# A fused attention and expert kernel: one exponential moved a pair sooner, the second pair's operands copied in three pieces, doubled filler products, and a new instruction order

## The chip, the cores and the metric

The kernel runs on one core of one Trainium2 chip. The metric is the time in microseconds (us) of one execution on the device, lower is better. The core's engines run side by side: TensorE (PE in the profile, with its weight loads as PEld), VectorE (DVE), ScalarE (ACT), GpSimd (POOL), and SyncE (SP), which issues DMAs. Results of products land in PSUM, in eight banks.

## The reference

Two steps, one behind the other. First soft-capped attention over 8 batches, 12 heads, 448 positions and 64 columns a head; then, on its output, four attention experts of 64 columns, of which each position uses two.

```python
def _attn_ref(q, k, v, cap):
    scores = np.matmul(q, k.transpose(0, 1, 3, 2)) / np.sqrt(64)
    scores = cap * np.tanh(scores / cap)              # cap = 30
    attn = softmax(scores)
    return np.matmul(attn, v)

def _moe_ref(x, w_gate, wq, wk, wv, wo):              # x: 8 x 448 x 768
    logits = x @ w_gate                               # 4 experts, the best 2 are used
    for e in range(4):
        a = softmax(causal(x @ wq[e] @ (x @ wk[e]).T / 8))
        ye = a @ (x @ wv[e]) @ wo[e]
        out += weight_of_e(logits) * ye
    return out
```

## The kernel before

**Attention** works on pairs of heads: 48 pairs (`NP`), six a batch (`HP`), and two more short ones (`NPV` is 50) for the last 128 positions of the last batch. For each pair the loop at the end of the kernel issues, in this order: loads (L486 keys, L495 queries, L490 tails), casts to 16 bits (`cast`, on POOL mostly), transposes on TensorE with one copy out of PSUM (`tr`, L711 and L701, copied at L752), score products (`fill`, L789 and L799), tanh on ACT (`tanh`, L842), one exp on ACT for all scores of a pair (`expo`, L854), products with the values (`pv`, L869 and L877), scaling on DVE, and a transpose into `xT`.

The scores of a pair come in three groups: X (three banks), Y1 and Y2 (the same two banks). A pair's tanh order is X, Y1, then the exp of the pair before, then Y2. Where a pair is not in `alone`, its Y2 products and the next pair's X products are one block in TensorE's order; a pair in `alone` gives them singly.

**The experts** of a batch are interleaved with the attention of the next batch: values, keys and queries (`b_v`, `b_qk`), the gate on POOL, two masks, and for each of the two chosen ranks a slot: score products and one exp of 1024 columns on ACT (`b_score`, L1158 and L1167), products with the values (`b_pv`, L1217, scaled on DVE at L1232), then sums on POOL (`b_ot`, L1242), transposes by DMA (L395) and output products (`b_wo`, L1279), stored at L1293. `exps` says which pair carries a slot: pairs 5 and 6 after a batch's first, and for batch 6 pairs 5 and 7, that is pairs 47 and 49. The last batch's experts (`last`, `last2`) follow at the end.

**The order** of each engine's instructions is worked out before anything is issued. Every operation is entered into a graph with an assumed duration and, in places, a due time counted from a tanh of ACT (`ref` and an offset). `solve` then simulates all engines and picks, on the engine that can start first, the operation with the lowest rank: its due time, changed by constants and by a jitter from `SEEDS` and `JIT`. Operations marked `first` (scores, transposes, operand copies) may pass ahead of the picked one when they are due soon. `LAND` is the time that the simulation assumes for a load to land. ACT's tanh and exp are chained in program order.

**Filler products** (L1589 at the start, L1644 behind each tanh of pairs 1 to 7) multiply zeros into a free bank.

Of the kernel before, what the change touches and what calls it, by code (L numbers as in the profile page):

```python
# [16 lines left out]
SWITCH = 0.1  # L17
WARM = 5.5
TAIL = 4
LAND = 2.942  # L20
LAND0 = 2.314
FLIGHT = 8
JIT = 0.377
SEEDS = (0, 0, 0, 641, 0, 564, 447, 0, 424, 0, 460, 0, 235, 957, 407, 782, 983, 0, 912, 404, 0, 970, 362, 0, 379, 864, 0, 72, 966, 0, 904, 104, 0, 980, 497, 974, 196, 827, 159, 0, 805, 165, 0, 235, 0, 755, 596, 262, 998, 26, 102, 0, 0, 552, 777, 594, 0, 873, 143, 97, 0, 0, 943, 0, 690, 925, 0, 147, 0, 0, 0, 830, 464, 0, 0, 0, 267, 0)
TWIRE = 0.1
BEGIN = {"POOL": 0.8, "DVE": 0.9, "SP": 0.8, "ACT": 0.8, "PE": 1.25}
NWARM = 6
KEEP = 8
KEEPN = 1
HEAD = 12.0  # L30
MD = 4
NAT = 36
# [21 lines left out]
class Graph:  # L54
# [79 lines left out]
    def solve(self, when, banks, lent):  # L134
# [44 lines left out]
        while len(order) < n:  # L179
            best = None  # L180
            for e, rs in ready.items():
                if not rs:
                    continue
                c = [(est(o, e), o) for o in rs if e == o.eng or not left]
                if not c:
                    continue
                t0 = min(x[0] for x in c)
                if t0 >= INF or (best is not None and t0 >= best[0]):
                    continue
                def rank(x):  # L190
                    u = x[1]
                    if u.name[:4] == "gexp":
                        return -INF, 0.0, 0
                    d = u.due + lag if u.first or left < TAIL else max(u.due + lag, t0 + 1.097)
                    d -= 0.796 * (u.grp is not None and not u.opens and left >= TAIL)
                    k = SEEDS[int(t0 / 4.0)] if t0 < 4.0 * len(SEEDS) else 0
                    if k:
                        d += ((u.idx * 40503 + k * 9973) % 1009 / 1009.0 - 0.5) * JIT
                    return d - 2.0 * (u.half == 1 and half == 1), u.due, u.idx

                near = t0 + (0.005 if left >= TAIL else SWITCH + 0.02)
                t, o = min((x for x in c if x[0] <= near), key=rank)
                early = e == "POOL" and t < HEAD
                if (e in ("PE", "DVE") or early) and not o.first:
                    for t2, u in c:
                        if u.first and u.due + lag < t + o.occ + 0.433 and t2 < t + (
                                o.occ if early else max(SWITCH + 0.01, min(o.occ, 0.25))):
                            t, o = t2, u
                            break
                if best is None or t < best[0]:  # L210
                    best = (t, e, o)
# [64 lines left out]
def kernel(  # L276
# [418 lines left out]
    def tr(p):  # L695
# [19 lines left out]
        if p == 0:  # L715
            gk, gq = Group(AUX), Group(AUX)
            pe(0, lambda: tk(gk, (1, 0, 2)), kr, [("tps", p, "k")], gk, occ=0.165, name=f"trk{p}")
            act(0.37, lambda: nc.scalar.copy(qk[t][:, S + 128 :], bank16(gk)[:, S + 128 : S + 512]),
                [("tps", p, "k")], [("qk", t, "k")], gk, fixed=True)
            pe(0, lambda: tq(gq, 0, 2), [("q16", i), "ident"], [("tps", p, "q")], gq, occ=0.1,  # L720
               name=f"trq{p}")
            pe(0, lambda: tq(gq, 2, 4), [("q16b",), "ident"], [("tps", p, "r")], gq, occ=0.1,
               name=f"trr{p}")
            dve(c_dve(S, True), lambda: nc.vector.tensor_copy(
                qk[t][:, 0:S], bank16(gq)[:, 0:S]), [("tps", p, "q"), ("tps", p, "r")], [("qk", t, "q")], gq,
                name="qk0")
            return
        g = Group(AUX)
        if p >= KD:
            pe(0, lambda: tq(g, 0, 2), [("q16", i), "ident"], [("tps", p, "q")], g, occ=0.1,  # L730
# [12 lines left out]
        pe(0, lambda: tk(g, (0, 1, 2)), kr + [("s", XB[0])] * (p == 1), [("tps", p, "k"), ("qkw", t)], g, occ=0.165, name=f"trk{p}")  # L743
        m, kx = (4, (-1,)) if p == 1 else (2, ())
        pe(0, lambda: (tq(g, 0, m), None if kx else tk(g, (-1,))),
           [("q16", i), "ident"] + (ktr if not kx else []),
           [("tps", p, "q")], g, occ=0.2 if kx else 0.15, name=f"trq{p}",
           due=5.0 if p == 1 else None)
        pe(0, lambda: tk(g, kx) if kx else tq(g, 2, 4), [("q16", i), "ident"] + (ktr if kx else []),
           [("tps", p, "r")], g, occ=0.06 if kx else 0.1, name=f"trr{p}" if p == 1 else "", due=5.0 if p == 1 else None)  # L750
        dve(c_dve(S + 512, True),
            lambda: nc.vector.tensor_copy(qk[t], bank16(g)[:, 0 : S + 512]),  # L752
            [("tps", p, x) for x in "kqr"], [("qk", t, "k"), ("qk", t, "q"), ("qk", t, "t")], g, name=f"qk{p}")
# [72 lines left out]
        return [o for o in G.ops if o.fixed][-1]  # L826

    XOFF = (5, 6)
    late = {6: (5, 7)}
    exps = {HP * (b + 1) + o: (b, s) for b in range(LB) for s, o in enumerate(late.get(b, XOFF))}  # L830
    alone = {0, *exps}
    ACTS = {}
    SL = {"X": (0, 3), "Y1": (3, 5), "Y2": (5, 7)}

# [148 lines left out]
    def b_v(b, ref):  # L983
        x = b % 2
        for n in range(4):
            g = Group(AUX + XB, 1.8)
            w = WIN[n]
            for j0 in (0, 2, 4):
                def mm(g=g, w=w, j0=j0):
                    for j in (j0, j0 + 1):  # L990
                        nc.tensor.matmul(  # L991
                            bank(g)[:, 0 : E * Dh + E], xT[x][:, j, w : w + 128], wvg[:, j, :],
                            start=(j == 0), stop=(j == NDC - 1),
                        )

                pe(0, mm, [("xT", x, j) for j in range(NDC)] + [("wvg", e) for e in range(E + 1)],
                   [("vps", b, n)], g, occ=0.22, name=f"v{b}_{n}",
                   due=(ref, 7.244 + 1.4 * n))
            lo = 64 if n == 3 else 0
            dve(0.08, lambda g=g, n=n: nc.vector.tensor_copy(  # L1000
                lg[x][:, (n + 1) % 4, :], bank(g)[:, E * Dh : E * Dh + E]),
# [6 lines left out]
    def b_qk(b, ref):  # L1008
        x = b % 2
        for r in range(2):  # L1010
            for which in "kq":
                g = Group(AUX + XB, 2.4)
                w2 = (wq2 if which == "q" else wk2)[r]
                for j in range(NDC):
                    def mm(g=g, w2=w2, j=j, which=which):
# [7 lines left out]
                    pe(S, mm, ([("mB", 0), ("mB", 1)] if which == "q" and b >= MD else []) + [("xT", x, i) for i in range(NDC)] + [  # L1023
                            (f"w{which}2", 2 * r), (f"w{which}2", 2 * r + 1)],
                        [(which, b, r)], g, name=f"{which}{b}_{r}",
                        due=(ref, 11.984 + 5.015 * r + 1.8 * (which == "q")))
                if which == "k":
                    dve(c_dve(S), lambda g=g, r=r: nc.vector.tensor_copy(
                        kB[x][r], bank(g)[:, 0:S]), [("k", b, r)], [("kB", x, r)], g, name=f"kB{b}")
# [334 lines left out]
    def last(ref):  # L1364
# [82 lines left out]
        for n in range(3):  # L1447
# [5 lines left out]
            def mm(g=g, n=n):  # L1453
                for e in range(E):
# [8 lines left out]
                ("vB", x, c) for c in range(n + 1)], [("pvL", n)], g, occ=0.12 * (n + 1),  # L1463
                name=f"pvL{n}")
            normed(n, g, view, ("pvL", n), (z[:, n].rearrange("p (e o) -> p e o", o=1),
                   [(b, 3, "z")]), None, WIN1[n], (ref, 9.616))
        last2(ref)

    def gate_tail(b, tag, g, ps, m, z, l, t, s_, key):
# [42 lines left out]
    def last2(ref):  # L1512
# [63 lines left out]
        for e in range(E):  # L1576
            pe(0, lambda e=e: pv_(e), [("p2", e), "vL"] + [("vB", x, c) for c in range(3)],
               [("pvL", 3)], g, occ=0.12, name="pvL3")
        normed(3, g, view, ("pvL", 3), (gt2[0].rearrange("p o e -> p e o"), [(b, 2, "z"), (b, 2, "s")]),
               gt2[3][:, 1, 0], W1, (ref, 9.108))  # L1580

# [14 lines left out]
    for p in range(NPV):  # L1596
# [13 lines left out]
        for what in order:  # L1610
            if what == "Y2" and p:
# [1 line left out]
                if p in exps:  # L1613
                    b_score(*exps[p])
                pv(p - 1)
                xt(p - 1, (ACTS["Y1", p], 3.335))
                if p % HP == 0 and p < NP:
                    bb = p // HP - 1
                    b_v(bb, ACTS["Y1", p])
# [88 lines left out]
```

## Time and profile before

| | |
|---|---|
| median of 3 runs | 306.69 us (305.9 to 307.45) |
| profiled execution | 306.74 us |
| its span, first to last instruction | 304.7 us |
| busy: ACT, PE, DVE, POOL | 290.8, 278.8, 212.0, 184.3 us |
| DMA | 53.12 MB, mean 174 GB/s |

Engines' busy times are unions over their instructions. A row of the timeline gives start, duration, engine, line, operation, output and input, with the count of merged instructions behind an x and, in brackets, the idle time of that engine before it and what ended it. L842 stands for line 842 of the kernel before. The chain of waits is followed back from the last instruction.

### The profile page before, as it was taken

How to read it: one execution, taken by the hardware profiler on the slowest of the kernel's cores; microseconds unless marked ns; L12 is line 12 of the kernel's file. 1: busy time of each engine (PE TensorE's matmuls, PEld its weight loads, DVE VectorE, ACT ScalarE, POOL GpSimd, SP SyncE). 2: the span in 40 equal slices, each digit the busy share in tenths (PEclk: the TensorE clock that was granted, in tenths of full speed). 3: DMA queues.
4: the chain of work that ended last, by engine and by line, in shares of the span. 5: the costliest groups of instructions: out<-in, count | busy, mean ns of one | idle time of the engine just before them, and what ended most of it. 6: DMA issues, size and time to landing. Idle time of an engine off the chain costs nothing.

```text
span 304.7 us, 8981 instructions
## 1 busy us (share of the span) xinstructions
PE 278.8 (92%) x3488; PEld 187.7 (62%) x3488; DVE 212.0 (70%) x643; ACT 290.8 (95%) x246; POOL 184.3 (61%) x513
## 2 busy tenths in 40 slices
PE   7886679999999999999999999999998889999993
PEld 3553446676657776667666676556665566667761
DVE  2354656776658886687867876688865887586883
ACT  5999999999999999999999999999999999999682
POOL 6696244899859674967689463945568332920420
PEclk9999999999999999999999999999999999999999
DMA  6799999999993599559995662539137950553127
GB/s 184 167 239 229 238 268 255 237 254 228 250 271 79 170 258 250 131 149 308 254 219 149 219 198 62 129 88 238 25 63 71 208 131 20 81 163 93 37 103 261
DMA packets 86874, 53.12 MB, mean 174 GB/s; under 512 B 47536, under 2 KB 83120, under 8 KB 86832
## 3 DMA queue, kind: packets, MB, share of 16 engines
q1 hardware_dynamic: 86528, 52.33, 68.9%
q8 instruction: 27, 0.44, 0.6%
q10 hardware_dynamic: 304, 0.23, 0.2%
q14 instruction: 15, 0.12, 0.2%
HBM read 36.19 MB, written 11.01 MB: 155 GB/s over the span
## 4 chain that ended last, share of the span: by engine, by line
ACT 83%; PE 7%; issue 3%; DMA 2%; DVE 1%; SPq 1%; POOL 1%; DVEq 0%; ACTq 0%; POOLq 0%
ACT yp L842 42%; ACT yp L854 37%; ACT pP L1167 5%; DMA kf<-in_k_dram 2%; PE A L1279 1%; PE Y0s L1518 0%; PE A L1345 0%; PE A L1372 0%; PE Y L789 0%; SPq L490 0%; PE X0X1s L1158 0%; SPq L495 0%; SPq L486 0%; PE X0s L1401 0%; PE A L1401 0%
## 5 line engine op out<-in xcount | busy, mean ns | idle before, releaser
L854 ACT ACTIVATE yp<-yp 128x3136 f16<-128x3136 f16 (+4 forms) x51 | 142.7, 2801 | 0.0
L842 ACT ACTIVATE yp<-Y 128x896 f16<-128x896 f32 (+2 forms) x100 | 101.7, 1017 | 1.1 <-PE Y L789 1.1
L842 ACT ACTIVATE yp<-X 128x1344 f16<-128x1344 f32 (+2 forms) x50 | 68.5, 1370 | 0.4 <-PE X L799 0.4
L877 PE MATMUL A<-v,yp 128*128 128x65 f16 x1116 | 55.5, 193 | 0.0
L877 PEld LDWEIGHTS <-yp 128*128 128x128 f16 x1116 | 48.4, 97 | 5.6 <-issue 3.7
L869 PE MATMUL A<-vtz,yp 128*128 128x130 f16 x186 | 41.3, 222 | 7.9 <-ACT yp L854 4.7
L901 DVE TENSOR_TENSOR xk<-A,rca 128x256 f16<-128x256 f32 (+1 forms) x96 | 39.5, 414 | 2.5
L651 POOL CAST q<-qf 112x512 f16<-112x512 f32 x44 | 26.7, 618 | 9.4 <-PE A L701 6.3
L687 POOL CAST v<-vf 128x384 f16<-128x384 f32 x48 | 24.3, 509 | 10.7 <-PE A L877 6.4
L898 DVE RECIPROCAL rca<-A 128x4 f32<-128x4 f32 (+1 forms) x96 | 17.1, 178 | 19.5 <-PE A L877 17.9
L869 PEld LDWEIGHTS <-yp 128*128 128x128 f16 x186 | 18.0, 97 | 20.5 <-ACT yp L854 9.3
L383 DVE COPY ob<-A 128x384 f32<-128x384 f32 (+1 forms) x50 | 26.4, 553 | 5.8 <-PE A L1279 5.1
L752 DVE COPY qk<-A 128x960 f16<-128x960 f16 x33 | 21.2, 653 | 10.0 <-PE A L701 8.5
L789 PE MATMUL Y<-qk 64*128 64x448 f16 x136 | 24.7, 357 | 2.3 <-ACT yp L842 1.7
L1232 DVE SCALAR_TENSOR_TENSOR oB<-A,rcb,mw 128x256 f16<-128x256 f32 x54 | 25.1, 479 | 1.1
L1279 PE MATMUL A<-wo,oT 128*128 128x384 f16 x108 | 24.2, 326 | 1.4 <-DVE ob L383 0.6
L636 POOL CAST k<-kf 128x384 f16<-128x384 f32 x33 | 16.6, 514 | 14.4 <-DMA kf<-in_k_dram 10.2
L1177 POOL TENSOR_SCALAR_AFFINE_SELECT pP<-pP 128x384 f16<-128x384 f16 x14 | 7.4, 527 | 29.4 <-ACT pP L1167 20.2
L1217 PE MATMUL A<-vB,pP 128*128 128x260 f16 x134 | 22.0, 274 | 0.9 <-DVE oB L1232 0.4
L701 PE MATMUL A<-ident,q 112*128 112x112 f16 x192 | 20.8, 212 | 1.5 <-POOL q L651 0.6
L991 PE MATMUL A<-wvg,xT 128*128 128x260 f16 x168 | 21.9, 274 | 0.0
L1242 POOL TENSOR_TENSOR oS<-oB,oB 128x512 f16<-128x512 f16 x14 | 16.2, 1154 | 6.1 <-issue 4.3
(231 smaller groups left out, 591.8 us busy)
## 6 DMA issues: line engine op xcount, KB each, us to landing
qf<-in_q_dram SPq DMA_DIRECT2D x23, 448.0 KB, 6.5
kf<-in_k_dram SPq DMA_DIRECT2D x23, 384.0 KB, 5.8
vf<-in_v_dram SPq DMA_DIRECT2D x23, 384.0 KB, 4.8
out_dram<-ob SPq DMA_DIRECT2D x21, 384.0 KB, 3.1
ktf<-in_k_dram SPq DMA_DIRECT2D x46, 32.0 KB, 5.3
vtf<-in_v_dram SPq DMA_DIRECT2D x46, 32.0 KB, 4.5
out_dram<-ob SPq DMA_DIRECT2D x6, 192.0 KB, 3.1
ob<-in_moe_wv_dram SPq DMA_DIRECT2D x2, 384.0 KB, 4.5
```

Of the source, the lines that this page charges most:

```text
L383: (nc.scalar.copy if o.eng == "ACT" else nc.vector.tensor_copy)(dst(), src())
L651: e(q16[i], qf[s][:, h].rearrange("p h (c d) -> p c h d", c=QC))
L687: nc.gpsimd.tensor_copy(v16[u][:, :, :, 0:Dh], vf[s][:, h].rearrange("p h (c d) -> p h c d", c=KC))
L789: nc.tensor.matmul(dst[:, g, o], kT[r, 128 * (c + 1) : 128 * (c + 2)], t[r, qs], start=True, stop=True,)
L842: ACTS[what, p] = act(c_act(n * (b - a)), lambda: nc.scalar.activation(y[:, a:b, 0:n], src[:, 0 : b - a, 0:n], AF.Tanh, scale=isc / capf), ...
L854: act(c_act(n * (b - a), False), lambda a=a, b=b, n=n: nc.scalar.activation(y[:, a:b, 0:n], y[:, a:b, 0:n], AF.Exp, scale=capf), ks, ks, f ...
L869: nc.tensor.matmul(ps[:, n, :, :], y[:, 2 * S + w : 2 * S + w + 128], vtz[u], start=(n == 0), stop=False, skip_group_check=True,)
L877: nc.tensor.matmul(ps[:, n, h, :], y[:, o : o + 128], v16[u][:, h, c, :], start=False, stop=(c == 2), skip_group_check=True,)
L901: dve(c_dve(128 * m), lambda g=g, i=i, rc=rc, m=m: nc.vector.tensor_tensor(xk[p % NXK][:, 2 * i : 2 * i + m, :, :], view(g)[:, 0:m, :, 0:D ...
L1217: nc.tensor.matmul(bank(g)[:, 0 : E * (Dh + 1)], pB[pi][:, o : o + 128], vB[x][:, c, :, :], start=(t == 0), stop=(t == len(cs) - 1),)
L1232: dve(c_dve(E * Dh) + 0.06, lambda g=g, k_=k_, n=n: nc.vector.scalar_tensor_tensor(oB[s][:, n, :, :], view(g)[:, :, 0:Dh], rcb[k_][:, 0, : ...
L1279: nc.tensor.matmul(bank(g)[:, 0 : D // 2], oT[x][:, n // 2, r, n % 2, :], wo2[r][:, c0:c1], start=(r == 0), stop=(r == 1),)
```

## The change

- `late` is empty, so batch 6's second slot is carried by pair 48 instead of pair 49.
- Pair 1's transposed keys, queries and tail keys go to three PSUM groups and are copied by three instructions (384, 448 and 128 columns) instead of one of 960.
- Pair 1 is in `alone`: its Y2 scores are a block of their own, as are pair 2's X scores.
- Behind each tanh of pairs 1 to 7 there are two zero products instead of one.
- The planner's constants change: the assumed landing time, jitter and seeds, the floors and bonuses of the rank, the window in which operations compete, the margin by which `first` operations pass (0.433 to 0.0), and the due offsets of several steps.

```diff
-LAND = 2.942
+LAND = 3.605
-JIT = 0.377
-SEEDS = (0, 0, 0, 641, 0, 564, ...)
+JIT = 0.518
+SEEDS = (0, 0, 783, 0, 707, 932, ...)
-KEEPN = 1
+KEEPN = 2
...
-                    d = u.due + lag if u.first or left < TAIL else max(u.due + lag, t0 + 1.097)
-                    d -= 0.796 * (u.grp is not None and not u.opens and left >= TAIL)
+                    d = u.due + lag if u.first or left < TAIL else max(u.due + lag, t0 + 0.998)
+                    d -= 1.869 * (u.grp is not None and not u.opens and left >= TAIL)
...
-                    return d - 2.0 * (u.half == 1 and half == 1), u.due, u.idx
+                    return d - 4.585 * (u.half == 1 and half == 1), u.due, u.idx
-                near = t0 + (0.005 if left >= TAIL else SWITCH + 0.02)
+                near = t0 + (0.0 if left >= TAIL else SWITCH + 0.02)
...
-                        if u.first and u.due + lag < t + o.occ + 0.433 and t2 < t + (
+                        if u.first and u.due + lag < t + o.occ + 0.0 and t2 < t + (
...
+        if p == 1:
+            for a, z_, fn, r_, y, o_ in (
+                    (S + 128, S + 512, lambda g: tk(g, (0, 1, 2)), kr + [("s", XB[0])], "k", 0.165),
+                    (0, S, lambda g: tq(g, 0, 4), [("q16", i), "ident"], "q", 0.2),
+                    (S, S + 128, lambda g: tk(g, (-1,)), ["ident"] + ktr, "t", 0.06)):
+                g = Group(AUX)
+                pe(0, lambda g=g, fn=fn: fn(g), r_, [("tps", p, y), ("qkw", t)], g, occ=o_,
+                   name=f"tr{y}{p}", due=5.0)
+                dve(c_dve(z_ - a, True), lambda g=g, a=a, z_=z_: nc.vector.tensor_copy(
+                    qk[t][:, a:z_], bank16(g)[:, a:z_]), [("tps", p, y)], [("qk", t, y)], g,
+                    name=f"qk{p}")
+            return
...
-    late = {6: (5, 7)}
+    late = {}
-    alone = {0, *exps}
+    alone = {0, 1, *exps}
...
-                   due=(ref, 7.244 + 1.4 * n))
+                   due=(ref, 3.186 + 1.4 * n))
-                        due=(ref, 11.984 + 5.015 * r + 1.8 * (which == "q")))
+                        due=(ref, 15.662 + 2.786 * r + 4.756 * (which == "q")))
-                   [(b, 3, "z")]), None, WIN1[n], (ref, 9.616))
+                   [(b, 3, "z")]), None, WIN1[n], (ref, 11.197))
-               gt2[3][:, 1, 0], W1, (ref, 9.108))
+               gt2[3][:, 1, 0], W1, (ref, 11.253))
-                xt(p - 1, (ACTS["Y1", p], 3.335))
+                xt(p - 1, (ACTS["Y1", p], 3.268))
-                        b_wo(bb, ACTS["Y1", p], *((19.451, 1.8) if bb < LB - 1 else (10.566, 0.5)))
+                        b_wo(bb, ACTS["Y1", p], *((22.44, 1.8) if bb < LB - 1 else (21.554, 0.5)))
```

More of the change, by code (lines that the diff above doesn't have):

```diff
@@ L19 @@
 TAIL = 4
-LAND = 2.942
+LAND = 3.605
 LAND0 = 2.314
 FLIGHT = 8
-JIT = 0.377
-SEEDS = (0, 0, 0, 641, 0, 564, 447, 0, 424, 0, 460, 0, 235, 957, 407, 782, 983, 0, 912, 404, 0, 970, 362, 0, 379, 864, 0, 72, 966, 0, 904, 104, 0, 980, 497, 974, 196, 827, 159, 0, 805, 165, 0, 235, 0, 755, 596, 262, 998, 26, 102, 0, 0, 552, 777, 594, 0, 873, 143, 97, 0, 0, 943, 0, 690, 925, 0, 147, 0, 0, 0, 830, 464, 0, 0, 0, 267, 0)
+JIT = 0.518
+SEEDS = (0, 0, 783, 0, 707, 932, 0, 0, 257, 546, 464, 19, 961, 813, 0, 0, 413, 216, 0, 651, 156, 222, 576, 59, 858, 0, 29, 0, 369, 488, 0, 391, 9, 0, 515, 944, 0, 0, 0, 856, 829, 438, 952, 853, 0, 301, 365, 0, 0, 796, 0, 0, 0, 0, 0, 0, 667, 105, 298, 0, 57, 906, 343, 666, 341, 0, 0, 0, 17, 725, 0, 886, 989, 0, 263, 684, 102, 483)
 TWIRE = 0.1
@@ L742, in tr @@
             return
[L743 to L750, printed above, removed]
+        pe(0, lambda: tk(g, (0, 1, 2)), kr, [("tps", p, "k"), ("qkw", t)], g, occ=0.165, name=f"trk{p}")
+        pe(0, lambda: (tq(g, 0, 2), tk(g, (-1,))), [("q16", i), "ident"] + ktr,
+           [("tps", p, "q")], g, occ=0.15, name=f"trq{p}")
+        pe(0, lambda: tq(g, 2, 4), [("q16", i), "ident"], [("tps", p, "r")], g, occ=0.1)
         dve(c_dve(S + 512, True),
```

## The prediction

> **What bounds the kernel now.** I read the page first: busy times, then the slices, then the shares of the chain that ended last.
>
> ```profile
> span 304.7 us, 8981 instructions
> ACT  5999999999999999999999999999999999999682
> PEclk9999999999999999999999999999999999999999
> ACT 83%; PE 7%; issue 3%; DMA 2%; DVE 1%; SPq 1%; POOL 1%; DVEq 0%; ACTq 0%; POOLq 0%
> ```
>
> ScalarE (ACT) is full from the second slice to the 37th and carries 83% of the chain. TensorE's granted clock is full in every slice. So the run has three stages: a head before ACT is full, a middle that lasts as long as ACT's own instructions, and a tail after ACT's last exponential. The ends of the middle, from the chain in order of time (first and third line) and the timeline (second):
>
> ```profile
> 14.32 2.91 ACT yp L842 x3
> 282.20 2.63 ACT L854 ACTIVATE yp<-yp 128x1920 f16<-128x1920 f16 x2
> 299.05 0.34 PE A L1345 x2
> ```
>
> From 14.32 nearly every piece of the chain is ACT's tanh (L842) or exp (L854). The last exp runs until 284.83 (282.20 + 2.63); TensorE's last output product ends near 299.4, and the span, with the last stores, at 304.7. The tail is 304.7 - 284.83 = 19.9 us. The change leaves ACT's middle instructions alone in number and shape, so it can pay only in the head, the tail, or through stalls of ACT that a new order makes or removes.
>
> **Head: the second pair's operands, copied singly.** The timeline of the head:
>
> ```profile
> 5.11 0.39 DVE L724 COPY qk<-A 128x448 f16<-128x448 f16 x1 [0.47 <-PE A L701]
> 5.42 0.22 DVE L761 COPY qk<-A 128x128 f16<-128x128 f16 x1
> 6.97 0.36 PE L701 MATMUL A<-ident,q 112*128 112x112 f16 x4
> 7.56 0.23 PE L711 MATMUL A<-ident,ktz 128*128 128x128 f16 x1
> 7.83 0.66 DVE L752 COPY qk<-A 128x960 f16<-128x960 f16 x1 [0.95 <-PE A L711]
> 8.56 0.36 PE L789 MATMUL X<-qk 64*128 64x448 f16 x2
> 6.77 1.28 ACT L842 ACTIVATE yp<-X 128x1344 f16<-128x1344 f32 x1
> 7.94 0.92 ACT L842 ACTIVATE yp<-Y 128x896 f16<-128x896 f32 x1
> 9.26 1.29 ACT L842 ACTIVATE yp<-X 128x1344 f16<-128x1344 f32 x1 [0.39 <-PE X L799]
> ```
>
> Pair 1 now has one copy of 960 columns. It starts at 7.83, once the tail keys are transposed (7.56 + 0.23), and ends at 8.49; the score products start at 8.56, and ACT sits idle 0.39 us before its tanh at 9.26. Split, the queries' copy need not wait for the tail keys: its transposes end at 7.33, a copy of that width took 0.39 for pair 0, so it ends near 7.75. The keys' copy (384 columns, between the 0.22 and the 0.39 of the rows above) lies before that, while queries are being transposed; the tail's (0.22 after 7.79) ends near 8.01. The next limit is the bank: pair 0's tanh of X ends at 8.05 (6.77 + 1.28). So the products start near 8.10 instead of 8.56: 0.46 sooner. ACT could begin from about 8.8, so nearly its whole wait goes; I take 0.42. The two more copies add fixed costs on DVE, about 0.39 + 0.22 + 0.35 - 0.66 = 0.3 us, hidden because DVE was waiting 0.95 us just there.
>
> **Head: pair 1 is no longer fused.** Making pair 1 "alone" issues its third score group (Y2) by itself instead of with pair 2's X.
>
> ```profile
> 14.26 0.36 PE L789 MATMUL X<-qk 64*128 64x448 f16 x2
> 11.24 2.82 ACT L854 ACTIVATE yp<-yp 128x3136 f16<-128x3136 f16 x1
> 14.32 0.92 ACT L842 ACTIVATE yp<-Y 128x896 f16<-128x896 f32 x1 [0.26 <-PE Y L789]
> 15.13 1.28 ACT L842 ACTIVATE yp<-X 128x1344 f16<-128x1344 f32 x1
> 10.46 0.95 POOL L636 CAST k<-kf 128x384 f16<-128x384 f32 x2 [2.10 <-DMA kf<-in_k_dram]
> 12.83 0.53 POOL L681 CAST ktz<-ktf 128x128 f16<-128x128 f32 x2
> ```
>
> ACT waits another 0.26 us at 14.32. Alone, Y2 of pair 1 can be filled during the exp at 11.24, so this wait goes as well; ACT would be some 0.7 to 0.8 early by then (consecutive ACT rows overlap by about 0.1, so a visible wait of 0.26 is a loss of about 0.37). But what is late next is pair 2's X: its products, behind its copy, start at 14.26 and tanh cannot start before about 14.95, against 15.13 now. That alone would cap the head's gain at 0.18. It holds only while the tail-key cast stays at 12.83 on POOL, 1.4 us behind the end of the key casts (10.46 + 0.95 = 11.41), memsets lying between. POOL idles 2.10 us before 10.46, and the planner's assumed landing time rises from 2.942 to 3.605, which invites it to put such memsets into that idle stretch. If it does, pair 2 comes sooner and the gain stays near 0.8. Between 0.18 and 0.8 I take 0.6.
>
> **Two zero products behind each tanh of pairs 1 to 7.** There were 21; 42 are now issued.
>
> ```profile
> 23.27 0.60 PE L1644 MATMUL A<-warm 128*128 128x512 f16 x2
> 20.79 0.36 PE L789 MATMUL Y<-qk 64*128 64x448 f16 x2
> 21.78 0.95 ACT L842 ACTIVATE yp<-Y 128x896 f16<-128x896 f32 x1
> 25.48 0.10 PEld L869 LDWEIGHTS <-yp 128*128 128x128 f16 x1 [2.10 <-ACT yp L854]
> ```
>
> Two products in a row took 0.60 us, so one more costs TensorE at most 0.30, and 21 more 6.3 us. All of it can hide: a Y group filled at 20.79 is done at 21.15 and is wanted at 21.78, 0.63 us later, and TensorE's weight loads waited 2.10 us for ACT at 25.48. If that cover is gone the price is at most 6.3 us; a gain is excluded for the profiled execution, since its clock is full already. I take zero, the nearest rows being the 0.63 and the 2.10.
>
> **Batch 6's second slot a pair sooner.** The slot is score products, one exp of 0.9 us on ACT (L1167), and behind it masks on POOL, ten products with the values (L1217), four reciprocals and scalings on DVE, two sums on POOL, two DMA transposes on SP, and the output products (L1279).
>
> ```profile
> 273.82 2.12 ACT L854 ACTIVATE yp<-yp 128x2240 f16<-128x2240 f16 x1
> 280.50 1.11 ACT L1167 ACTIVATE pP<-X0X1s 128x1024 f16<-128x1024 f32 x1
> 282.99 0.22 PE X1s L1217 x2
> 283.62 0.11 PE A L1217
> 284.18 0.53 PE X1s L1217 x4
> 284.95 0.33 PE A L1217 x3
> 285.96 2.52 SPq L395 DMA_TRANSPOSE oT<-oS  x2
> 291.78 0.50 PE L1279 MATMUL A<-wo,oT 128*128 128x384 f16 x2
> 270.00:284.80 14.80, 13.92 (x208) 10.20 (x205) 10.95 (x41) 14.80 (x15) 1.55 (x5) 1.00 0.30 94
> 284.80:299.50 14.70, 14.65 (x181) 9.98 (x177) 11.87 (x48) 9.77 (x26) 4.88 (x9) 1.00 0.34 120
> ```
>
> The last two lines are the windows view: length, then busy time of TensorE, its weight loads, DVE, ACT and POOL, and the clock. The exp at 280.50 moves to behind the exp of pair 47, which ends near 275.9, so about 4.6 us forward (ACT's order changes, its sum does not, so the last exp still ends where it did). The ten value products lie in the chain at 282.99 to 285.28 and take 0.22 + 0.11 + 0.53 + 0.33 = 1.19 us of it. A pair sooner they lie ahead of the last exp, where TensorE idles at least 14.80 - 13.92 = 0.88 us, against 0.05 behind it. DVE's part of the slot leaves the stretch in which it was 11.87 of 14.70 busy, SP's two transposes (2.52 us of its queue, ahead of the final stores) go earlier, and two PSUM banks come free sooner. The six output groups, which could not start before 291.78, may start near 287; but the change also sets their due time later relative to the tail, so I credit none of their cost. The tail's gain lies between 0 (the same work merely reordered) and 1.19 plus six groups' worth of room; I take 1.1, the measured chain pieces less a little.
>
> The Trainium skill (Perfetto Trace Analysis, Identifying the Most-Contended Engine) says that matmul busy time is a poor measure of TensorE's headroom and that the busy share of weight loads is the better one. By matmul busy time the earlier window has 0.88 us of room and the slot's gain would be 0.9; by weight loads (10.20 of 14.80) there is room for all 1.19. The trace bears the page out in part: the four products at 284.18 occupy 0.53 us of chain.
>
> **The order searched anew.** Ranking constants, jitter and seeds reorder PE, DVE, POOL and SP. The middle has nothing to regain that can be seen, and something to lose:
>
> ```profile
> 100.00:200.00 100.00, 97.14 (x1233) 67.59 (x1233) 76.14 (x226) 100.00 (x76) 70.85 (x182) 1.00 0.71 193
> ```
>
> ACT is busy for 100.00 of these 100 us. Rows overlap by 0.1, which hides stalls of that size: a gain of at most 14 x 0.1 = 1.4 us if each of the 14 slots of the batches had one. A loss is open upwards, and its price stands with the rivals. I take zero.
>
> **Sum.** 0.6 (head) + 1.1 (tail) = 1.7 us. The profiled execution took 306.74, its span plus 2.04 around it; 306.74 - 1.7 = 305.04, given as 305.0. The three runs have a median of 306.69, so the profiled one is typical, and no correction is made. What a measurement of this kernel can tell from no change is about 0.5%, 1.53 us: faster is below 305.16, slower above 308.22.
>
> **Rivals.**
>
> *The stores hold the end.* The output leaves late and together.
>
> ```profile
> 299.50:304.70 5.20, 0.20 (x2) 0.00 (x0) 0.93 (x2) 0.07 (x1) 0.00 (x0) 0.98 0.71 243
> ```
>
> After 299.5 TensorE is done and the DMA engines are still 0.71 busy. If the later due time keeps batch 6's output products as late as now, its stores still queue up with batch 7's and the tail's 1.1 is lost: 306.74 - 0.6 = 306.1. For it: the due time moves to 21.554 from a reference only a pair sooner. Against: the list scheduler fills an idle TensorE with whatever is ready. Chance 0.21.
>
> *The output groups rise too.* If they fill holes from 287 on, their time leaves the end with their stores: one group's two products took 0.50 at 291.78, six groups are at most 3.0 us, and I credit three quarters, since the products of neighbours overlap: 305.0 - 2.2 = 302.8. For it: the operands are there 4 us sooner. Against: TensorE is idle for only 0.05 us there, so there are few holes. Chance 0.17.
>
> *Scores come later and ACT starves (slower).* The look-ahead by which score products pass ahead of other work falls from 0.433 to 0.0.
>
> ```profile
> 271.72 0.34 PE L789 MATMUL X<-qk,kd 64*128 64x128 f16 x6 [0.28 <-ACT pP L1167]
> 272.10 1.18 ACT L842 ACTIVATE yp<-X 128x1152 f16<-128x1152 f32 x1
> ```
>
> Behind an exp of a slot the next X group starts when the banks come free, and tanh starts 0.04 us after it: no slack. There are 14 slots. If at each one a product group of about a third of a microsecond (the pair of 448-column products at 20.79 took 0.36) goes first, 14 x 0.33 = 4.6 us are lost: 305.0 + 4.6 = 309.6. It cancels the gain from 0.12 us a slot (1.7 / 14) and makes a measured loss from 0.23. Against: due times keep a margin of 0.1 for each step between engines. Chance 0.26, of which 0.23 lies above 308.22.
>
> *The early copies bring nothing* because pair 2 is late, and only 0.18 of the head is gained: 306.74 - 0.18 - 1.1 = 305.5, inside the forecast's own range.
>
> **How the numbers follow.** Forecast 0.36, two thirds of it (0.24) below 305.16; stores 0.21 and groups 0.17 on one side each. Faster: 0.24 + 0.17 = 0.41. Same: 0.12 + 0.21 + 0.03 = 0.36. Slower: 0.23. The forecast's own range is 304.2 to 305.9. The range of 8 in 10 runs from 302.8, the groups' case, to 309.0, inside the slower one.
>
> **What would show it.** Right: no wait of ACT before the tanh of pair 1's X, pair 1's Y2 directly behind the first exp, the last exp ending near 284.2, the slot's exp near 275, its value products before 281, and the last TensorE product near 297.7. Wrong: ACT rows in the middle with starts further apart than now, above all behind the slots' exps; or a last exp as late as before; or stores still draining for as long after a TensorE that finishes sooner.

## The result and the profile after

| | before | after |
|---|---|---|
| median of 13 runs each | 306.62 us (305.9 to 307.45) | 308.04 us (307.62 to 309.76) |
| profiled execution | 306.74 us | 308.04 us |
| its span | 304.7 us | 306.0 us |

After stands to before as 1.0049, with a 95% interval of 1.0031 to 1.0068: slower by 1.4 us, where 1.7 us less had been forecast. The size is near the edge of what can be told from no change; measured once more, in another comparison, it came out at 1.0048 (1.0034 to 1.0061).

The page after: span, two of the 40-slice rows, and the shares of the chain that ended last.

```profile
span 306.0 us, 9028 instructions
ACT  5999999999999999999999999999999999999670
PEclk9999999999999999999999999999999999999996
ACT 85%; PE 6%; issue 4%; DVE 2%; DMA 1%; ACTq 0%; DVEq 0%; POOL 0%; POOLq 0%
```

ACT fills as many slices as before. From the tanh of pair 2's X to the end of the last exp it takes 269.7 us before (15.13 to 284.83) and 269.5 after (14.87 to 284.36). So the middle has not grown, and the question is the head or the tail. From L789 on the lines stand 8 further down than before: L842 is now L850, L854 is L862, L1167 is L1175, L1279 is L1287, L1345 is L1353, and the stores at L1293, L1354, L1358 and L1361 are L1301, L1362, L1366 and L1369. The timeline of the head (start, length, engine, line, and in brackets the wait ahead of it):

```profile
6.53 0.92 ACT L850 ACTIVATE yp<-Y 128x896 f16<-128x896 f32 x1 [1.39 <-PE Y L797]
7.34 1.28 ACT L850 ACTIVATE yp<-X 128x1344 f16<-128x1344 f32 x1
9.38 1.29 ACT L850 ACTIVATE yp<-X 128x1344 f16<-128x1344 f32 x1
11.36 2.82 ACT L862 ACTIVATE yp<-yp 128x3136 f16<-128x3136 f16 x1
14.07 0.92 ACT L850 ACTIVATE yp<-Y 128x896 f16<-128x896 f32 x1
14.87 1.30 ACT L850 ACTIVATE yp<-X 128x1344 f16<-128x1344 f32 x1
8.33 0.23 PE L711 MATMUL A<-ident,ktz 128*128 128x128 f16 x1
8.60 0.23 DVE L736 COPY qk<-A 128x128 f16<-128x128 f16 x1 [0.55 <-PE A L711]
8.68 0.37 PE L797 MATMUL X<-qk 64*128 64x448 f16 x2
```

The wait of 0.39 before pair 1's X (now at 9.38) is gone, and so is the 0.26 before pair 1's Y2 (14.07 instead of 14.32); pair 2's X starts 0.26 sooner, at 14.87 instead of 15.13. But the first wait did not go because the products came sooner. The very first tanh is 0.58 late (6.53 instead of 5.95), since POOL waited 1.25 us instead of 0.53 for the load of pair 0's tail keys, and pair 1's X products start at 8.68 beside 8.56, behind pair 0's tanh of X, which ends only at 8.62 (7.34 + 1.28). When such a load lands differs from one execution to the next: with the old head, POOL's cast behind it starts at 4.69 in the profile before, and at 5.10 and 4.80 in two others. Two more traces show how little this pair of profiles tells of the head. First the kernel before with an untouched head (`e3_before_no_stores6` below), then the kernel after with an untouched head (`e1_last_store`):

```profile
6.38 0.92 ACT L842 ACTIVATE yp<-Y 128x896 f16<-128x896 f32 x1 [0.83 <-PE Y L789]
9.39 1.29 ACT L842 ACTIVATE yp<-X 128x1344 f16<-128x1344 f32 x1
14.88 1.30 ACT L842 ACTIVATE yp<-X 128x1344 f16<-128x1344 f32 x1
```

```profile
6.12 0.92 ACT L850 ACTIVATE yp<-Y 128x896 f16<-128x896 f32 x1 [0.83 <-PE Y L797]
9.38 1.29 ACT L850 ACTIVATE yp<-X 128x1344 f16<-128x1344 f32 x1 [0.35 <-PE X L807]
```

With a late first tanh the old head has no wait before pair 1's X either, and with an early one the new head still waits 0.35. Over the traces, pair 2's X starts at 15.13, 14.88, 15.35 and 15.10 with the old head, and at 14.87, 15.01, 15.41, 14.76, 14.80 and 14.81 with the new one and all its zero products (a seventh, at 16.38, is not counted: there TensorE was slow early in the head, with 0.55 us for a product with pair 0's tail keys that took 0.36 in the others). The means differ by some 0.2 us, less than executions of one head differ among themselves. The times in the trace of an execution of 644 us, where others of its kernel took 307, are left out here and below.

The timeline of the end of the middle, and three windows (length, busy time of TensorE, weight loads, DVE, ACT, POOL, then clock, share of the DMA engines, GB/s):

```profile
275.29 1.08 ACT L1175 ACTIVATE pP<-X 128x1024 f16<-128x1024 f32 x1
281.82 2.54 ACT L862 ACTIVATE yp<-yp 128x1920 f16<-128x1920 f16 x2
270.00:284.80 14.80, 14.35 (x220) 10.82 (x219) 11.83 (x44) 14.37 (x15) 3.52 (x6) 1.00 0.32 91
284.80:299.50 14.70, 13.63 (x165) 9.04 (x161) 11.80 (x43) 10.29 (x26) 2.84 (x8) 1.00 0.29 109
16.00:270.00 254.00, 239.34 (x2999) 161.99 (x2997) 182.48 (x541) 254.00 (x196) 165.17 (x435) 1.00 0.74 181
```

The slot's exp went from 280.50 to 275.29, the last exp ends at 284.36 instead of 284.83, and from 284.8 to 299.5 TensorE has 13.63 us of work instead of 14.65. So up to here the change does what it was forecast to do, in part. What became of it shows in the last nine microseconds of the timeline: TensorE's and DVE's last pieces, then the stores that SP issues, in order.

```profile
297.58 0.49 PE L1353 MATMUL A<-wo,oTL 128*128 128x384 f16 x2
297.91 0.81 PE L1287 MATMUL A<-wo,oT 128*128 128x384 f16 x4
298.43 1.02 DVE L383 COPY ob<-A 128x384 f32<-128x384 f32 x2
294.84 0.35 SPq L1301 DMA_DIRECT2D out_dram<-ob  x1
296.06 0.34 SPq L1369 DMA_DIRECT2D out_dram<-kf  x1
296.83 0.33 SPq L1301 DMA_DIRECT2D out_dram<-ob  x1
297.31 0.35 SPq L1369 DMA_DIRECT2D out_dram<-kf  x1
297.96 0.49 SPq L1366 DMA_DIRECT2D out_dram<-kf  x1
298.54 0.72 SPq L1362 DMA_DIRECT2D out_dram<-kf  x1
299.32 1.40 SPq L1369 DMA_DIRECT2D out_dram<-kf  x1
300.81 0.54 SPq L1301 DMA_DIRECT2D out_dram<-ob  x1
```

TensorE's last piece and the same stores before:

```profile
298.89 0.81 PE L1345 MATMUL A<-wo,oTL 128*128 128x384 f16 x4
294.36 2.95 SPq L1293 DMA_DIRECT2D out_dram<-ob  x3
297.74 0.33 SPq L1361 DMA_DIRECT2D out_dram<-kf  x1
298.70 0.33 SPq L1354 DMA_DIRECT2D out_dram<-kf  x1
299.59 0.33 SPq L1361 DMA_DIRECT2D out_dram<-kf  x1
300.46 0.48 SPq L1358 DMA_DIRECT2D out_dram<-kf  x1
300.99 0.59 SPq L1361 DMA_DIRECT2D out_dram<-kf  x1
```

Before, batch 6's three large stores (`ob`, 384 KB each) left first and batch 7's followed. After, the third of them is the very last. Its rows are ready at 299.45 (298.43 + 1.02), but SP is still issuing a store of 1.40 us, so it goes out at 300.81, 1.36 us later. One more store, of half a tile's columns, goes out from ACT's queue, at 299.15 before and 298.61 after. TensorE ends at 298.72 (297.91 + 0.81) instead of 299.70 (298.89 + 0.81); the span ends 1.3 us later. Counted from the end of the last exp, TensorE's last product ends 14.87 us on before and 14.36 after; from there to the end of the last packet of output, in the traces' packets, it is 3.7 us before (to 303.36) and 5.9 after (to 304.64); the 1.3 us from there to the end of the span are the same. The rate of the DMA engines, in 40 equal slices of 292 to 306 us, first before, then after:

```profile
GB/s 0 0 0 0 0 47 0 0 0 351 413 413 413 421 228 9 184 421 413 404 395 404 347 369 377 408 413 369 281 202 246 360 27 0 0 0 0 0 0 0
GB/s 0 0 0 0 0 0 0 0 0 0 202 421 413 106 395 377 421 404 413 421 421 404 307 202 158 158 386 369 325 325 255 272 360 220 105 26 0 0 0 0
```

A slice is 0.35 us, and both rows move the same outputs. Before, the rate is near 400, save for a gap in which no output was ready (9) and a dip near the end (202). After, the drain starts a slice later and ends three slices later; its dip (158) comes where the two half-height stores leave (L1366 and the one that took 1.40 us to issue), and a second, milder one (255) follows while the last stores are out together.

### The profile page after: what moved, and what is told of

Its sections match the earlier page's. It is cut to its first block, busy times and chain, and to the rows that moved or that the text cites. A ratio compares the mean times of both kernels' runs of the same rounds, so it can differ in the third digit from the quotient of the medians.

```text
span 306.0 us, 9028 instructions
## 1 busy us (share of the span) xinstructions
PE 281.0 (92%) x3509; PEld 189.8 (62%) x3509; DVE 211.6 (69%) x644; ACT 290.9 (95%) x247; POOL 183.4 (60%) x513
## 4 chain that ended last, share of the span: by engine, by line
ACT 85%; PE 6%; issue 4%; DVE 2%; DMA 1%; ACTq 0%; DVEq 0%; POOL 0%; POOLq 0%
ACT yp L850 43%; ACT yp L862 37%; ACT pP L1175 5%; DMA ktf<-in_k_dram 1%; PE A L1026 1%; PE A L1287 1%; PE A L1353 1%; PE Y L797 0%; PE A L885 0%; PE X L1166 0%; PE A L1409 0%; PE A L1526 0%; PE A L877 0%; PE A L1580 0%; DVE xk L972 0%
## 5 line engine op out<-in xcount | busy, mean ns | idle before, releaser
L862 ACT ACTIVATE yp<-yp 128x3136 f16<-128x3136 f16 (+4 forms) x51 | 141.7, 2781 | 0.0
L850 ACT ACTIVATE yp<-Y 128x896 f16<-128x896 f32 (+2 forms) x100 | 100.7, 1007 | 1.4 <-PE Y L797 1.4
L850 ACT ACTIVATE yp<-X 128x1344 f16<-128x1344 f32 (+2 forms) x50 | 67.6, 1353 | 0.0
L1240 DVE SCALAR_TENSOR_TENSOR oB<-A,rcb,mw 128x256 f16<-128x256 f32 x55 | 25.4, 480 | 1.4
L636 POOL CAST k<-kf 128x384 f16<-128x384 f32 x33 | 16.4, 506 | 15.2 <-PE A L711 7.7
L1287 PE MATMUL A<-wo,oT 128*128 128x384 f16 x108 | 23.9, 326 | 0.4
L760 DVE COPY qk<-A 128x960 f16<-128x960 f16 x32 | 20.4, 652 | 3.1 <-PE A L701 2.8
L939 DVE COPY xT<-A 128x448 f16<-128x448 f16 (+1 forms) x38 | 14.6, 385 | 9.3 <-PE A L930 9.2
L999 PE MATMUL A<-wvg,xT 128*128 128x260 f16 x168 | 20.9, 274 | 0.0
L701 PE MATMUL A<-ident,q 112*128 112x112 f16 x192 | 19.5, 213 | 0.6 <-DVE oB L1240 0.3
```

The source lines that it names most:

```text
L850: ACTS[what, p] = act(c_act(n * (b - a)), lambda: nc.scalar.activation(y[:, a:b, 0:n], src[:, 0 : b - a, 0:n], AF.Tanh, scale=isc / capf), ...
L862: act(c_act(n * (b - a), False), lambda a=a, b=b, n=n: nc.scalar.activation(y[:, a:b, 0:n], y[:, a:b, 0:n], AF.Exp, scale=capf), ks, ks, f ...
L1240: dve(c_dve(E * Dh) + 0.06, lambda g=g, k_=k_, n=n: nc.vector.scalar_tensor_tensor(oB[s][:, n, :, :], view(g)[:, :, 0:Dh], rcb[k_][:, 0, : ...
L1287: nc.tensor.matmul(bank(g)[:, 0 : D // 2], oT[x][:, n // 2, r, n % 2, :], wo2[r][:, c0:c1], start=(r == 0), stop=(r == 1),)
```

## The experiments

Two theories. **A:** the output stores set the end; the output groups of batch 6 got so late a due time (21.554) that their third store is issued last, and what TensorE saves is waited for there. **B:** the loss lies upstream, in starved ACT or in the head, and the stores only follow.

**Batch 6's third store cut to one row** (128 rows become one; the order is kept, and the other 127 rows of the output are left out).

```diff
-            sp(lambda ...: nc.sync.dma_start(out[b, w + lo : w + 128, :], o[lo:128, :]),
+            sp(lambda ...: nc.sync.dma_start(out[b, w + 127 : w + 128, :], o[127:128, :]) if b == LB - 1 and n == 2
+               else nc.sync.dma_start(out[b, w + lo : w + 128, :], o[lo:128, :]),
```

> The changed kernel, order untouched; of batch 6's third store (384 KB, issued last at 300.81) only one row of 128 is written, so that output is left out. Theory A (the output stores' drain sets the end, and this store leaves last): the last landing, seen by SP at 304.99, falls back to that of the store before it, about 304.0; time 307.0, a fall of 0.8 to 1.4 us from 308.04. Theory B (the time was lost ahead of the last exp, by a first tanh at 6.53 instead of 5.95 and by waits of tanh behind the slots' exps): no change beyond 0.3 us, 307.8 to 308.2.

Measured: 306.69 us, ratio to before 0.9999 (0.9976 to 1.0021). One store of 384 KB carries 1.35 us of the 1.4, as theory A has it and theory B has not. Whether its place or its bytes count, this run alone does not tell.

**All three of batch 6's stores cut to one row,** in the kernel after and in the kernel before (the same diff without `n == 2`).

> The changed kernel, order untouched; of each of batch 6's last three stores one row is written, so 1.15 MB of the output are left out. Theory A: at 0.41 MB a microsecond that is 2.8 us less to drain; the end is then set by the last batch's own output products, which end near 298.1 instead of 299.4 before, so the time is 305.0 to 305.6. Theory B: 307.5 to 308.1, since work ahead of the stores is unchanged.

> The kernel before, order untouched, the same three stores cut to one row each (1.15 MB of the output left out). Theory A: here these stores go first and the drain is less in the way: a fall of 0 to 1.0 us, to 305.6 to 306.6, so that it ends no sooner than the changed kernel without them. Theory B: no change, 306.4 to 306.7, and the changed kernel without them stays 1.2 us slower.

Measured: after 305.93 us (0.9986, 0.9972 to 1.0001); before 306.42 us (1.0005, 0.9992 to 1.0018). The stores cost the kernel after 2.1 us, and the kernel before at most 0.2, less than can be told from nothing. So it is their place that costs, not their bytes. The kernel after came out 0.3 us above theory A's range; the kernel before lies in both theories' ranges, and theory B's for the kernel after is missed by 1.6. What is left between the two without the stores is 0.5 us, and the two intervals touch. The traces show as much in the tail: from the end of the last exp to TensorE's last product it is 14.35 us in the kernel after and 14.89 in the kernel before.

**Stores earlier in the kernel after:** due times of the tail and the seeds from 272 us on are changed, so that batch 7's first stores go first, batch 6's three follow in a row, and a half-width store of batch 7 is the last; before 272 us the order is the same.

```diff
-  [(b, 3, "z")]), None, WIN1[n], (ref, 11.197))
+  [(b, 3, "z")]), None, WIN1[n], (ref, 7.41))
-  gt2[3][:, 1, 0], W1, (ref, 11.253))
+  gt2[3][:, 1, 0], W1, (ref, 12.766))
-  b_wo(..., (21.554, 0.5))
+  b_wo(..., (18.325, 1.2))
```

> The changed kernel with other due times for the output products of the last two batches (18.325 with steps of 1.2, 7.41 and 12.766 in place of 21.554, 11.197 and 11.253) and other seeds from 264 us on, so that four of the last batch's stores leave some 2 us sooner and no 384 KB store leaves last. Everything before 264 us keeps its order. Theory A: the DMA queue no longer holds the end; 305.0 to 306.5. Theory B: 307.7 to 308.3, since nothing ahead of 264 us is changed.

Measured: 306.01 us, 0.9989 (0.9977 to 1.0001). All of the loss is gone with nothing but the tail's order changed, and all outputs written. TensorE even ends later, 15.2 us behind the last exp instead of 14.36, yet the last packet is out at 302.60 instead of 304.64. Theory B, which forecast 307.7 at least, falls.

**One due time alone,** 21.554 to 16.5.

> The changed kernel with one constant changed: the due offset of batch 6's output products 16.5 instead of 21.554, so that its three stores go ahead of the last batch's (as in the kernel before) and none is issued last. Order unchanged before 272 us. Theory A (a 384 KB store of batch 6 that leaves last sets the end): 306.2 to 307.2. Rival C (the amount to be drained at the end sets it, in whatever order): 307.7 to 308.3, because as many bytes still leave in the last 9 us.

Measured: 307.29 us, 1.0014 (0.9993 to 1.0036): 0.75 of the 1.4 us comes back from this one constant. That is 0.1 above theory A's range and 0.4 below that of rival C, which came up here: that the amount still to be written at the end counts, in whatever order. The order of issue is as intended, batch 6's three stores ahead of all of batch 7's. What else is needed for the rest, of the due times and seeds that the run before changed as well, was not told apart.

**The slot back at pair 49,** everything else of the change kept, the tail's due times set for early stores as above (19.153, 1.2; 6.271; 11.605).

```diff
-    late = {}
+    late = {6: (5, 7)}
```

> The kernel of the fourth experiment (stores earlier) with the slot put back to pair 49, its due times and seeds from 264 us on chosen anew for it (19.153 with steps of 1.2, 6.271, 11.605). It tells what the slot's move is worth once the stores are out of the way. If the move shortens the tail as forecast (1.1 us), this is slower than the fourth experiment by 0.6 to 1.2 us: 306.6 to 307.2. If the move brings nothing, the two are equal within 0.2: 305.8 to 306.2.

Measured: 306.43 us, 0.9983 (0.996 to 1.0006); with the slot moved it was 306.01 us and 0.9989. The time lies between the two ranges, and the ratios, each to the kernel before measured beside it, put neither ahead: what the move is worth is below what these runs can tell. The due times were also chosen anew for each, so they are not all that differs. The timelines show where a gain goes. With the slot moved (first two lines) and with it at its old place (last two), TensorE's last product and SP's last store:

```profile
298.63 0.82 PE L1353 MATMUL A<-wo,oTL 128*128 128x384 f16 x4 [0.51 <-ACT oTL L383]
299.75 0.33 SPq L1362 DMA_DIRECT2D out_dram<-kf  x1
```

```profile
299.49 0.82 PE L1353 MATMUL A<-wo,oTL 128*128 128x384 f16 x4 [0.46 <-ACT oTL L383]
300.68 0.33 SPq L1362 DMA_DIRECT2D out_dram<-kf  x1
```

TensorE and the last issue are 0.9 us sooner with the move, and both spans are 304.2: from TensorE's last product to the last packet it is 3.1 us with the move and 2.4 without.

**One zero product instead of two behind each tanh of pairs 1 to 7,** order kept; the second is not issued.

> The changed kernel, order untouched, without the second zero product behind each tanh of pairs 1 to 7 (21 products left out, nothing moved into their place). If their cover holds, as forecast, 307.7 to 308.4, no change. If they stood in the way of scores, up to 1 us faster. If they keep the clock from falling, slower and with a lower granted clock between 10 and 55 us.

Measured: 308.74 us, 1.0077 (1.005 to 1.0105), an interval that overlaps that of the kernel after, from five executions between 307.91 and 310.14. The median lies 0.3 above the range for no change, and the sign for a falling clock did not come: from 10.4 to 55 us the windows view has a granted clock of 1.00. In this run's profile TensorE was slow early in the head, as in the seventh trace above (0.55 us for the same product), and the last exp ended at 286.47, so executions with such a start may be what raised the median; that is not shown. What the second product is worth stayed open, so both were taken out below.

**The kernel before, stores earlier** (`e8_before_stores`; due times 5.789, 11.158 and 19.081 for 9.616, 9.108 and 10.566; seeds behind 264 us).

> The kernel before with the same kind of due times as the fourth experiment (19.081, 5.789, 11.158 in place of 10.566, 9.616, 9.108) and seeds from 264 us on chosen for early stores: the last batch's stores leave first, batch 6's behind them, only half-row stores last. Theory A: the kernel before loses little to its stores, since its order already puts batch 6 first; 306.0 to 307.0, no sooner than the fourth experiment.

Measured: 305.85 us, 0.9979 (0.9961 to 0.9997), the lowest median of all and 0.15 below the range. The stores' order could be bettered before as well, by 0.6 us going by the ratio. It beats both kernels, though the kernel before by little, and "no sooner than the fourth experiment" (306.01, 0.9989) did not come: the two can't be told apart. With the stores in a good order, nothing is left to show for the rest of the change.

**The changed kernel again, and without any zero products,** side by side on one chip; in the second neither product is issued, the order is kept.

> The changed kernel once more, beside the kernel before and the next three on the same chip, so that their differences don't rest on runs of other days. Theory A (the end is set by the output stores, batch 6's third being issued last): about 308.0 us, ratio near 1.005, span near 306.0, last store issued by the scheduler of batch 6's rows near 300.8. A chance result of the first comparison would come out within 306.0 to 307.0.

> The changed kernel in the same order with neither of the two zero products behind the tanh of pairs 1 to 7; nothing else differs. If they cost nothing, as the prediction had it, the time stays at that of the changed kernel run beside it, within 0.6 us, and the stretch up to pair 8 takes as long. If they held up the scores (cover gone), it is faster by up to 28 x 0.22 = 6 us. If they keep the granted clock full while the work is thin, leaving them out shows half-speed stretches of 3.413 us in the first 30 us and a time up to 2 us longer.

Measured: 308.08 us (1.0048, 1.0034 to 1.0061) and 308.69 us (1.0065, 1.0049 to 1.0081). The windows view of both, 14 to 25 and 25 to 40 us, first with the zero products, then without:

```profile
14.00:25.00 11.00, 9.21 (x108) 5.29 (x106) 4.88 (x15) 11.00 (x10) 7.66 (x38) 1.00 0.95 235
25.00:40.00 15.00, 12.03 (x145) 7.02 (x146) 6.94 (x23) 15.00 (x13) 7.05 (x17) 1.00 1.03 246
```

```profile
14.00:25.00 11.00, 8.89 (x105) 5.37 (x105) 5.94 (x17) 10.26 (x9) 9.25 (x46) 0.84 0.94 216
25.00:40.00 15.00, 9.26 (x115) 6.21 (x116) 6.20 (x21) 14.91 (x13) 5.12 (x12) 0.87 1.02 242
```

Without them the granted clock falls to 0.84 and 0.87 in these stretches, and ACT, full with them (11.00 of 11.00), waits 0.74 us in the first. The clock over the span is 0.964 to 0.980 in all six executions without, 0.992 to 0.997 with. So the zero products keep the clock, and there is no sign that they hold anything up, though a small gain from their absence could hide behind the clock's loss. In time it is 0.6 us by the medians, and the two intervals overlap. The expectation's bound for lost cover is too low: it counts 28 products, and 42 are left out.

**The two half-height stores as one.** The tile behind L1366 and L1369 holds 64 rows of batch 6 and 64 of batch 7. Both go out as one store to a destination of two blocks, at the place of the first; in the kernel after, and in the kernel before with stores earlier.

```diff
-  sp(lambda: nc.sync.dma_start(out[LB - 1, KM:S, :], o[0:64, :]),
+  sp(lambda: nc.sync.dma_start(out.rearrange("b s d -> (b s) d")[(LB - 1) * S + 256 : (LB + 1) * S, :]
+     .rearrange("(t r) d -> t r d", t=2)[:, KM - 256 : S - 256, :], o[0:128, :]),
```

> The changed kernel in the same order, with the two half-height stores of the shared tile (64 rows of batch 6, 64 rows of batch 7) issued as one store of 128 rows to both places, at the place of the first. Theory A with the slow half-height stores as the cause of the drain's rate: the rate no longer falls to 160-230 kB/us for 1 to 1.5 us, one issue fewer stands ahead of batch 6's third store, and the end comes 0.5 to 1.4 us sooner: 306.6 to 307.5 beside 308.0. If the rate falls for another reason (the end of TensorE's work, memory, the queue count), no change: within 0.3 of the changed kernel.

> The kernel before with the stores brought forward (as in e8_before_stores, same order), and the two half-height stores in one. If both gains hold together: 305.0 to 305.6 us, ratio near 0.995, and no stretch of packets at half rate in the last 8 us. If after the stores have gone sooner the last outputs' arithmetic sets the end, the time stays at e8_before_stores' 305.9 (ratio near 0.998).

Measured: 314.78 us (1.0273, 1.0249 to 1.0297) and 312.74 us (1.0211, 1.0186 to 1.0237). Both expectations failed, by 7 us and in the other direction. The rate in 40 slices of 296 to 314 us, and the issues with their time to landing, of the kernel after in this form:

```profile
GB/s 0 0 48 437 382 191 410 382 410 423 410 389 345 338 167 72 44 99 276 317 157 75 48 55 48 55 55 48 55 55 48 55 55 44 51 55 20 0 0 0
out_dram<-kf SPq DMA_DIRECT2D x3, 384.0 KB, 2.7
out_dram<-kf SPq DMA_DIRECT2D x1, 192.0 KB, 11.5
```

The tail of the row stands at 44 to 55 GB/s for some 6 us: about an eighth of the full 410, or the rate of two of 16 engines. The Trainium skill (DMA: Bandwidth & Descriptors, Rules for kernel authors) says that an outermost dimension of fewer than 16 confines a DMA to at most that many engines; the destination here begins with a dimension of 2, and 2/16 of 410 is 51, an estimate by that rule. The rate in the trace agrees. The experiment says nothing on whether the half-height stores would be better merged; it changed the spread over the engines along with the height.

## Why the prediction was wrong

*What bounds the kernel.* Right for head and middle. The tail was named as "after ACT's last exponential" and then treated as TensorE's: the sum ended with its last product, and the 5 us of stores behind it were taken as a constant. They are not: 3.7 us from TensorE's last product to the last packet of output before, 5.9 after. (The prediction took the product's end, 299.39, from the chain; by the timeline it is 299.70. And the slot's exp, given as 0.9 us, is 1.11 in its row. The sum rests on neither.)

*The tail, the step that failed.* "The tail's gain lies between 0 (the same work merely reordered) and 1.19 plus six groups' worth of room; I take 1.1." From the last exp's end to the end of the span it is 21.6 us instead of 19.9: 1.7 more, where 1.1 less had been forecast. Of that, TensorE's part is 0.5 less, half of the 1.1, and the drain behind it 2.3 more. The lower end, 0, was wrong. A reordering can lose, because the order of output groups is the order of stores, and 384 KB issued last cost 1.35 us, by the run with that store cut to one row. The due time of 21.554 stood in the prediction as a reason to credit nothing, and was given no price; set back alone, it returns 0.75 us of the 1.4. What the slot's move alone did to the time is below what these comparisons can tell. The marks of this step came as forecast for the slot (its exp at 275.29 for "near 275", its value products ended by 281). The last exp's end at 284.36 for "near 284.2" is partly luck: the traces of the old head end it at 284.25 to 285.06, those of the new one counted above at 284.26 to 284.90. TensorE's mark missed (its last product at 298.72 for "near 297.7").

*The rival "the stores hold the end"* named the right mechanism, the right reason (the due time) and a chance of 0.21, but priced it as the lost gain only: 306.1, still faster than before. With the last store counted it is slower than before by 1.4. The sign named under "what would make it wrong", stores draining for as long after a TensorE that finishes sooner, came about, and more: 5.9 us instead of 3.7.

*The head.* Two signs came: no wait before pair 1's X, and Y2 directly behind the first exp. The first came by luck, with a first tanh 0.58 late; where the first tanh was early, the wait was still 0.35. Of the 0.6 some 0.2 is left over the traces, near the cap of 0.18 and not clear of their spread. One reason shows in `e1_last_store`: the queries' copy does go ahead of the tail keys', but pair 1's X products stand in TensorE's order behind the transpose of those keys (8.36 there, the products at 8.69, the one with the tail keys at 8.98), and POOL casts the tail keys at 8.01, where the traces of the old head have it at 7.08 to 7.21. The memsets' place on POOL, on which 0.6 rested, did not help: in the profile after, pair 2's tail keys are cast 1.6 us behind the end of the key casts (12.51 behind 10.95), before 1.4.

*Zero products.* Priced at zero, and no run shows a cost. "A gain is excluded for the profiled execution, since its clock is full already" looked at one execution in the old order. With one such product the clock was full in that profile, but in another of the same head (the kernel before, stores earlier) it was 0.50 from 22.0 to 25.4 us; in the new order it was full from 14 to 40 us with two and with one, and fell to 0.84 and 0.87 there with none.

*Scores come later and ACT starves,* with 0.26 the heaviest rival: not what happened. ACT was busy for 254.00 of 254 us from 16 to 270, and its stretch from pair 2's X to the last exp's end is 0.2 us shorter than before. That the change came out slower is not in its favour.

*The output groups rise too:* they didn't; two of batch 6's six are TensorE's last work (L1287 at 297.91), where the last of the six ended at 296.42 before.

*The range,* 302.8 to 309.0, held the time by luck: its upper end was set by the rival of a starved ACT, which was not the cause.

## What to carry to other kernels

Where a kernel ends in a queue of stores, price an edit of the tail by the last store's landing, not by the last product: list the stores with their sizes in the order in which they are issued, and ask which becomes last. A planner that counts a fixed time for each store (`lat=2.5` here) and nothing for the bytes ahead of it has no reason to avoid a large one at the end; set their due times so that no large one is last, and look at the list again after each reordering. A gain ahead of such a queue is lost in it unless the queue moves as well. And look at more than one trace before calling a wait gone: here the first tanh moved by up to 0.7 us between executions of one head (5.95 to 6.61).

## What the runs showed of the hardware

- The rate of the stores falls while the half-height ones leave. In the kernel after with stores earlier, the two of them are the last ones issued before a pause; the rows are SP's issues, and the rate in 40 slices of 292 to 306 us:

```profile
294.31 0.48 SPq L1366 DMA_DIRECT2D out_dram<-kf  x1
294.84 0.59 SPq L1369 DMA_DIRECT2D out_dram<-kf  x1
296.61 2.15 SPq L1301 DMA_DIRECT2D out_dram<-ob  x3
GB/s 0 0 0 0 0 272 395 413 386 421 360 281 184 211 404 176 421 413 299 421 413 413 421 421 154 373 364 243 9 18 4 0 0 0 0 0 0 0 0 0
```

From about 400 the rate goes down to 184 and 211 at 296.2 to 296.9 us, before the next store has data on the way. In the kernel after it goes down to 158 in the same way. There SP's issue of the second one took 1.40 us instead of 0.59 at the same time; that the slow drain held it up is likely and not shown. What in the chip lowers the rate was not found.
- A destination with an outermost dimension of 2 ran at about an eighth of the rate (44 to 55 GB/s), and a store that should have saved an issue cost 7 us.
- The granted clock falls in steps: without the zero products the clock's record has stretches at half speed of 3.413, 3.413 and 6.827 us from 15.7, 26.0 and 39.6 us, one length and its double. The Trainium skill (TensorE: Matmul & The Clock Gate, What's actually happening) gives a window of 4096 cycles, 3413 ns, and lets the clock drop after at least one idle window. The lengths agree; but the 3.41 us ahead of each drop were not idle here: TensorE was busy for 2.11, 1.60 and 1.07 of them, against 2.93, 2.67 and 2.61 in the same stretches with the zero products, where the clock stayed. ACT-bound as the kernel is, 13.7 us at half speed go with about 0.6 us by the medians, which is not clear of noise.
